# Exponentials of score tiles in two places by turns, and weight blocks loaded one tile earlier, in a fused attention and softplus-MLP kernel

## Chip, cores and metric

The kernel runs on one core of one Trainium2 chip. The metric is the device time of one launch in microseconds (us); lower is better. Engines are named as in the profile: PE is TensorE (matmuls and transposes), PEld its weight loads, DVE is VectorE, ACT is ScalarE, POOL is GpSimd, SP is the queue that issues all DMAs.

## What is computed

Attention over 8 batches with 8 heads, 576 positions and head width 64, in which scores more than `tau` below their row's maximum are dropped, and then a two-layer MLP with softplus over all 4608 tokens:

```python
scores = scale * q @ k.T                                  # per batch and head, 576 x 576
thresh = max(scores, axis=-1) - tau
attn   = softmax(where(scores >= thresh, scores, -1e9))
x      = (attn @ v) as (4608, 512)
h      = x @ w_in                                         # 512 -> 2048
g      = maximum(h, 0) + log1p(exp(-abs(h)))
out    = g @ w_out                                        # 2048 -> 512
```

`q`, `k`, `v` are float32; `w_in` and `w_out` arrive as 64-bit floats, and the kernel turns them into float32 pairs (a high and a low part) on the chip.

## The kernel before

**Attention.** There are 32 units, one for each batch and pair of heads, and each unit has 9 tiles of 128 rows of scores: 288 tiles in all, counted by `g`. A tile goes through these steps: `scores` (PE, 4 matmuls of 288 columns, 8 for the middle tile, into one of two pairs of PSUM banks), `row_max` (DVE, the negated maximum and the threshold), `exps` (ACT, line 435, from PSUM into `e_all`), `mask` (DVE, line 440: keeps what is over the threshold and sums the row), `weights_T` (PE, lines 471 to 477: transposes the masked exponentials), `weights_hi` and `weights_lo` (copies out of PSUM), and the products with `v`.

`e_all` has room for two tiles, its two halves; a tile takes the half of its parity. Tiles come in pairs (0 and 1, 2 and 3, 5 and 6, 7 and 8; tile 4 stands alone). The last 64 columns of a row of scores don't fill a block of 128. So the second tile of a pair transposes the middle 128 columns of `e_all`, which hold the remainders of both tiles, in one instruction (line 471), ahead of its own four (line 474). That instruction reads both halves. The exponentials of the next pair's first tile go into one of these halves, and so they come after it.

**The order.** The main loop walks the 288 tiles and writes out the steps of each by a string of letters. For the first 36 tiles it is `PAT0 = "RMTeShlfpfxvwp"`: row maximum of the next tile, mask of this one, transposes of this one, exponentials of the next, scores of the tile after that, and so on; `w` starts a block of weights, `v` issues three of the products with `v`, and each `p` is a point at which deferred work whose time has come is written out (two points to a tile). After that the string is `PAT`. The framework's planner then fixes the order of each engine's instructions by this order and by its own estimates of what is ready, so that an instruction can stand some tiles earlier on its engine than in the string. Every engine runs its instructions in that fixed order.

The first five units (`s.whole`, `NF = 5`) use float32 products of four passes with `v` (line 549) and need no low part, so they don't use the two buffers `gL`. MLP work (`f`) begins at tile 41; before that PE has only attention.

**Weights.** 32 blocks of 128 x 512 are loaded and split beside the first tiles. Block n is started at tile `int(W0 + n * W1)`, with `W1 = 2`: a load of 512 KB on SP (line 185) into pieces of a pool of 16; then, `WD` points later, line 193 on ACT (`first`), line 194 on POOL, lines 200, 202 and 205 on DVE some points apart, two steps on POOL (lines 125 and 132), and for `w_in` two stores to DRAM on SP (line 234).

Of the kernel before, what the change touches and what calls it, by code (L numbers as in the profile page):

```python
# [9 lines left out]
F32 = mybir.dt.float32  # L10
F32R = mybir.dt.float32r
# [12 lines left out]
P = 128  # L24
# [8 lines left out]
LAG0 = 5  # L33
PAT = "ThRlefmpfxSvwp"
PAT0 = "RMTeShlfpfxvwp"
WD = 2
ST = (1, 3, 4, 4, 5, 6, 6, 8)
VO = (1, 1, 1, 0)
RT = 1
# [12 lines left out]
NF = 5  # L52
TG = 36
W1 = 2.0
W0 = 1
SPA = 0


# [1 line left out]
def tile_kernel(ctx: ExitStack, tc: tile.TileContext, q, k, v, tau, w_in, w_out, out):  # L60
# [8 lines left out]
    nc = tc.nc  # L69
    B, H, S, D = q.shape  # L70
    NT, DM = out.shape
    DFF = w_in.shape[1]
    SM = 512
    SR = S - SM
    HS = S // 2
    NC = SM // P
# [8 lines left out]
    apool = ctx.enter_context(tc.tile_pool(name="apool", bufs=2))  # L85
# [11 lines left out]
    ident = identr.bitcast(F32)  # L97
# [52 lines left out]
    def to_f32(src, want, name, then):  # L150
# [29 lines left out]
        if src.dtype == F32:  # L180
            nc.sync.dma_start(m, src)
            later_(WD, lambda: then(parts, w, done))
            return
# [29 lines left out]

        later_(WD, first)

# [59 lines left out]
    for b in range(B):  # L275
        for kind in (("one", "two") if b < NSPLIT else ("all",)):
            for hp in range(NPAIR):
                s = Unit()
# [5 lines left out]
                for g, (j, members) in enumerate(groups):  # L284
                    c = 0
# [113 lines left out]

    e_all = cpool.tile([P, 2, S], F32, name="e_all")
    banks = [ps_s.tile([P, 2, 512], F32, tag="s", name=f"s_{i}") for i in range(SB)]
    nth = [0]

    def scores(s, t):
        if t == s.tiles[0]:
            s.sums = apool.tile([P, 9], F32, tag="sums", name=f"sums_{s.i}")
            s.half, s.sp, s.m, s.grp = {}, {}, {}, {}
        sp = banks[nth[0] % SB]  # L410
        s.half[t] = half = nth[0] % 2
        nth[0] += 1
        s.sp[t] = sp
        if t == NC:
            parts = [(qm[:, n, j, :], j) for j in range(2) for n in range(2)]
        else:
            j = 0 if t < NC else 1
            c = t if t < NC else t - NC - 1
            parts = [(s.qT[j][n][:, c * P:(c + 1) * P], j) for n in range(2)]
        k0 = (1 - half) * SR  # L420
        for m, (lhs, j) in enumerate(parts):
            for hf in range(2):
                i = nc.tensor.matmul(sp[:, hf, 0:HS], lhs, s.kT[j][:, k0 + hf * HS:k0 + (hf + 1) * HS],  # L423
                                     start=(m == 0), stop=(m == len(parts) - 1))
        scored.append(i)
# [6 lines left out]
        s.m[t] = (negm, thr)  # L432

    def exps(s, t):
        nc.scalar.activation(e_all[:, s.half[t], :].rearrange("p (h n) -> p h n", h=2), s.sp[t][:, :, 0:HS],  # L435
                             AF.Exp, bias=s.m[t][0], scale=1.0)

    def mask(s, t):
        e2 = e_all[:, s.half[t], :].rearrange("p (h n) -> p h n", h=2)
        masked.append(nc.vector.scalar_tensor_tensor(  # L440
            out=e2, in0=s.sp[t][:, :, 0:HS], scalar=s.m.pop(t)[1], in1=e2, op0=ALU.is_ge, op1=ALU.mult,
            accum_out=s.sums[:, s.tiles.index(t):s.tiles.index(t) + 1]))
# [8 lines left out]
    def mate(s, t):  # L451

        if t == NC:
            return None, False
        u = t if t < NC else t - 1
        return (t + 1, False) if u % 2 == 0 else (t - 1, True)

    def weights_T(s, t):
        half = s.half[t]
        e = e_all[:, half, :]  # L460
        other, second = mate(s, t)
        lone = other is None
        if 9 * NPAIR * s.b + 9 * s.hp + t < TG:
            main = ps_g.tile([P, NC, P], F32, tag="g", name=f"tm_{s.i}_{t}")
            rest = ps_g.tile([P, NC, P], F32, tag="g", name=f"tr_{s.i}_{t}")[:, 0, :] if lone or second else None
        else:
            sp = s.sp[t]
            main = sp[:, 0, :].rearrange("p (c n) -> p c n", n=P)
            rest = sp[:, 1, 0:P]
        if second:  # L470
            nc.tensor.transpose(rest, e_all.rearrange("p h n -> p (h n)")[:, SM:SM + P], ident)  # L471
        for c in range(NC):
            c0 = half * SR + c * P
            nc.tensor.matmul(main[:, c, :], e[:, c0:c0 + P], ident, is_transpose=True, start=True, stop=True)  # L474
        if lone:
            r0 = 0 if half else SM
            nc.tensor.transpose(rest[0:SR, :], e[:, r0:r0 + SR], ident)
        s.sp[t] = (main, rest)
# [358 lines left out]
    for kind, g in WL:  # L837
        for m in range(4):
            n = len(prep)
            prep.append((int(W0 + n * W1), prep_w_in if kind == "i" else prep_w_out,  # L840
                         (g, m) if kind == "i" else (4 * g + m,)))
# [69 lines left out]
    for n in (0, 2, 1):  # L911
        qkT(u0, 1, n)
        point()
    u0.eng, u0.eng_lo = eng, nc.gpsimd
    scores(*tiles[0])
    row_max(*tiles[0])
    exps(*tiles[0])
    scores(*tiles[1])
    for j in range(2):
        split_v(u0, j)  # L920
# [3 lines left out]
    for g, (cur, t) in enumerate(tiles):  # L924
# [5 lines left out]
        for step in PAT0 + ("m" if g == TG - 1 else "") if g < TG else PAT:  # L930
            if step == "T":
                weights_T(cur, t)
            elif step == "h":
                weights_hi(cur, t)
            elif step == "l":
                weights_lo(cur, t)
            elif step == "R" and nxt:
                row_max(*nxt)
            elif step == "e" and nxt:
                exps(*nxt)  # L940
            elif step == "m" and nxt:
                mask(*nxt)
            elif step == "M":
                mask(cur, t)
            elif step == "f":
                upto += quota / PAT.count("f")
                while done < upto:
                    done += next(ffn)
            elif step == "x":
                extras(cur.i, cur.tiles.index(t))  # L950
            elif step == "S" and g + 2 < NS:
                scores(*tiles[g + 2])
            elif step == "v":
                slow_products()
            elif step == "w":
                while prep and prep[0][0] <= g:
                    _, f, a = prep.pop(0)
                    f(*a)
            elif step == "p":
                point()  # L960
# [38 lines left out]
```

## Time and profile before

| | |
|---|---|
| median of 3 runs | 1451.85 us (1451.37 to 1452.93) |
| the profiled execution | 1450.65 us; span in the trace 1448.9 us |
| busy share of the span | PE 97%, DVE 68%, ACT 59%, POOL 41% |
| DMA moved | 189.93 MB, mean 131 GB/s |

The busy shares are means over the whole span. The first tenth of it, in which PE has only attention and the weights are prepared, differs from the rest, so the rows that matter are those of windows. PEclk is the clock that TensorE was granted, as a share of the full one.

### The profile page before, as it was taken

The numbers are of one execution on the slowest core, as the hardware profiler recorded it, in microseconds if no ns is written. First come the engines' busy times: TensorE is split into PE (matmuls) and PEld (weight loads), VectorE is DVE, ScalarE is ACT, GpSimd is POOL, SyncE is SP. The second block draws the span as 40 slices with busy tenths as digits, with TensorE's granted clock in tenths as the row PEclk, the third lists the DMA queues.
The fourth block names the chain that finished last, engine by engine and source line by source line (L and its number), as shares of the span: only waits on it lengthen the run. The fifth ranks groups of instructions, "written<-read, shape, count | busy, mean of one in ns | idle before, by whom it ended". The sixth has DMA issues, their size and how long they took to land.

```text
span 1448.9 us, 23497 instructions
## 1 busy us (share of the span) xinstructions
PE 1399.3 (97%) x7860; PEld 1161.6 (80%) x7860; DVE 983.1 (68%) x2211; ACT 848.1 (59%) x1615; POOL 591.0 (41%) x619
## 2 busy tenths in 40 slices
PE   6987999999999999999999999999999999999998
PEld 4654788878888888888888888888888888788886
DVE  6977688877777777777777777777777777402111
ACT  5766767767656566657665665667665765311010
POOL 3667666544333333344334333444334431324221
PEclk9999999999999999999999999999999999999999
DMA  5767765445333533444433533354344532344321
GB/s 160 220 192 231 212 187 170 138 121 154 109 102 110 137 115 110 119 134 150 123 111 96 153 106 101 116 151 120 113 119 136 148 98 74 101 130 129 119 85 44
DMA packets 131208, 189.93 MB, mean 131 GB/s; under 512 B 35312, under 2 KB 86800, under 8 KB 131088
## 3 DMA queue, kind: packets, MB, share of 16 engines
q1 hardware_dynamic: 131088, 188.43, 44.5%
q8 instruction: 63, 1.03, 0.3%
q14 instruction: 57, 0.47, 0.1%
HBM read 140.51 MB, written 27.41 MB: 116 GB/s over the span
## 4 chain that ended last, share of the span: by engine, by line
PE 78%; DVE 7%; ACT 5%; issue 3%; DMA 3%; POOL 2%; SPq 1%; POOLq 0%; ACTq 0%; DVEq 0%
PE s L423 10%; PE h L647 9%; PE h L645 9%; PE h L649 8%; PE o L707 8%; PE o L705 7%; PE s L474 7%; PE o L703 7%; PE pv L555 3%; PE pv L556 3%; PE tr L364 2%; DVE e_all L440 2%; DVE negm L430 2%; PE pv L549 1%; POOL g L132 1%
## 5 line engine op out<-in xcount | busy, mean ns | idle before, releaser
L132 POOL TENSOR_TENSOR g<-st,g 128x512 fp32r<-128x512 f32 x144 | 191.7, 1349 | 196.3 <-DVE g L129 182.5
L440 DVE SCALAR_TENSOR_TENSOR e_all<-s,thr,e_all 128x576 f32<-128x576 f32 x288 | 234.4, 815 | 53.0 <-ACT e_all L435 49.8
L430 DVE TENSOR_REDUCE negm<-s 128x1 f32<-128x576 f32 x288 | 217.1, 754 | 43.1 <-PE s L423 34.6
L435 ACT ACTIVATE e_all<-s,negm 128x576 f32<-128x576 f32 x288 | 215.9, 751 | 39.3 <-PE tr L471 20.7
L707 PE MATMUL o<-wo_o,g 128*128 128x512 f32 x576 | 232.3, 404 | 5.3 <-POOL g L132 5.3
L703 PE MATMUL o<-wo_o,g 128*128 128x512 f32 x576 | 232.0, 403 | 1.1 <-ACT st L667 0.7
L647 PE MATMUL h<-xl,wi 128*128 128x512 f32 x576 | 232.8, 404 | 0.0
L645 PE MATMUL h<-xh,wi 128*128 128x512 f32 x576 | 229.8, 399 | 0.0
L649 PE MATMUL h<-xh,wi 128*128 128x512 f32 x576 | 229.3, 398 | 0.0
L705 PE MATMUL o<-wo_o,g 128*128 128x512 f32 x576 | 228.5, 397 | 0.0
L498 ACT CAST gH<-s 128x512 fp32r<-128x512 f32 (+1 forms) x270 | 145.0, 550 | 139.1 <-PE s L474 135.6
L132 DVE TENSOR_TENSOR gL<-s,gH 128x512 fp32r<-128x512 f32 (+1 forms) x270 | 168.8, 634 | 47.8 <-ACT gH L498 25.3
L423 PE MATMUL s<-kT,qT 128*128 128x288 f32 x1024 | 192.2, 310 | 6.2 <-ACT gH L498 1.8
L423 PEld LDWEIGHTS s<-kT,qT 128*128 128x128 f32 x1024 | 148.5, 190 | 27.9 <-issue 11.3
L474 PE MATMUL s<-identr,e_all 128*128 128x128 f32 x1008 | 155.1, 276 | 4.8 <-DVE e_all L440 4.8
L129 DVE CAST g<-st 128x512 fp32r<-128x512 f32 x128 | 57.4, 485 | 149.5 <-ACT st L667 149.0
L667 ACT ACTIVATE st<-h 128x512 f32<-128x512 f32 x144 | 78.3, 596 | 115.3 <-PE h L649 114.6
L474 PEld LDWEIGHTS s<-identr,e_all 128*128 128x128 f32 x1008 | 114.7, 141 | 22.3 <-DVE e_all L440 12.6
L707 PEld LDWEIGHTS o<-wo_o,g 128*128 128x128 f32 x576 | 108.4, 188 | 29.1 <-POOL g L132 11.0
L645 PEld LDWEIGHTS h<-xh,wi 128*128 128x128 f32 x576 | 108.3, 188 | 23.5 <-issue 1.0
L703 PEld LDWEIGHTS o<-wo_o,g 128*128 128x128 f32 x576 | 108.5, 188 | 22.2 <-DVE g L129 2.0
L649 PEld LDWEIGHTS h<-xh,wi 128*128 128x128 f32 x576 | 108.4, 188 | 21.6
(107 smaller groups left out, 2366.4 us busy)
## 6 DMA issues: line engine op xcount, KB each, us to landing
wi<-wi_d SPq DMA_DIRECT2D x144, 512.0 KB
qT<-qT SPq DMA_DIRECT2D x124, 128.0 KB
R<-r_d SPq DMA_DIRECT2D x64, 144.0 KB
kn<-in_k_dram SPq DMA_DIRECT2D x32, 256.0 KB
qn<-in_q_dram SPq DMA_DIRECT2D x32, 256.0 KB
vn<-in_v_dram SPq DMA_DIRECT2D x32, 256.0 KB
wc_i<-in_moe_w_in_dram SPq DMA_DIRECT2D x16, 512.0 KB
wi_d<-wc_i SPq DMA_DIRECT2D x32, 256.0 KB
```

The lines of the kernel that those rows point to most:

```text
L132: eng.tensor_tensor(out=out_, in0=in_, in1=hi.bitcast(F32), op=ALU.subtract)
L423: i = nc.tensor.matmul(sp[:, hf, 0:HS], lhs, s.kT[j][:, k0 + hf * HS:k0 + (hf + 1) * HS], start=(m == 0), stop=(m == len(parts) - 1))
L430: nc.vector.reduce_max(negm, s.sp[t][:, :, 0:HS], axis=AX.XY, negate=True)
L435: nc.scalar.activation(e_all[:, s.half[t], :].rearrange("p (h n) -> p h n", h=2), s.sp[t][:, :, 0:HS], AF.Exp, bias=s.m[t][0], scale=1.0)
L440: masked.append(nc.vector.scalar_tensor_tensor(out=e2, in0=s.sp[t][:, :, 0:HS], scalar=s.m.pop(t)[1], in1=e2, op0=ALU.is_ge, op1=ALU.mult, ...
L474: nc.tensor.matmul(main[:, c, :], e[:, c0:c0 + P], ident, is_transpose=True, start=True, stop=True)
L645: nc.tensor.matmul(h, wi[:, 0, cc, :], u.h[cc], start=(cc == 0), stop=False)
L647: nc.tensor.matmul(h, wi[:, 0, cc, :], u.l[cc], start=False, stop=False)
L649: nc.tensor.matmul(h, wi[:, 1, cc, :], u.h[cc], start=False, stop=(cc == NCC - 1))
L703: nc.tensor.matmul(o, gh[:, sl], wo[fc][:, 0, :], start=(i == 0), stop=False)
L705: nc.tensor.matmul(o, gh[:, sl], wo[fc][:, 1, :], start=False, stop=False)
L707: nc.tensor.matmul(o, gl[:, sl], wo[fc][:, 0, :], start=False, stop=(i == QF - 1))
```

## The change

Three things change. The first five units put the exponentials of successive pairs by turns into `e_all` and into a second place, `e_more`, which takes one of the two `gL` buffers (`e_more` is used by units 0 to 4, `gL` from unit 5 on); each place still has two halves by parity, and mask and transposes read the place that the tile's exponentials went to. `W0` goes from 1 to 0, so that block n is loaded at tile 2n and not 2n + 1. `WD` goes from 2 to 4, so that it is taken up four points after its load and not two.

```diff
-WD = 2
+WD = 4
...
-W0 = 1
+W0 = 0
...
     e_all = cpool.tile([P, 2, S], F32, name="e_all")
+    e_more = apool.tile([P, NC, 320], F32R, tag="gL", name="e_more").bitcast(F32)
+    e_more = e_more.rearrange("p c n -> p (c n)")[:, 0:2 * S].rearrange("p (h n) -> p h n", h=2)
+    pairs = [0]
...
         sp = banks[nth[0] % SB]
         s.half[t] = half = nth[0] % 2
+        pairs[0] += not mate(s, t)[1]
+        s.e[t] = e_more if s.whole and pairs[0] % 2 else e_all
         nth[0] += 1
...
     def exps(s, t):
-        nc.scalar.activation(e_all[:, s.half[t], :].rearrange("p (h n) -> p h n", h=2), s.sp[t][:, :, 0:HS],
+        nc.scalar.activation(s.e[t][:, s.half[t], :].rearrange("p (h n) -> p h n", h=2), s.sp[t][:, :, 0:HS],
                              AF.Exp, bias=s.m[t][0], scale=1.0)
...
     def weights_T(s, t):
         half = s.half[t]
-        e = e_all[:, half, :]
+        e = s.e[t][:, half, :]
...
         if second:
-            nc.tensor.transpose(rest, e_all.rearrange("p h n -> p (h n)")[:, SM:SM + P], ident)
+            nc.tensor.transpose(rest, s.e[t].rearrange("p h n -> p (h n)")[:, SM:SM + P], ident)
```

`mask` reads `s.e[t]` in the same way.

## Rows read from the trace of the kernel before

**Rows 1.** The page, busy time of PE in the whole span.

```profile
PE 1399.3 (97%) x7860; PEld 1161.6 (80%) x7860; DVE 983.1 (68%) x2211; ACT 848.1 (59%) x1615; POOL 591.0 (41%) x619
```

**Rows 2.** Windows: stretch, length, busy time by engine, PEclk, DMA share, GB/s.

```profile
20.00:134.00 114.00, 98.11 (x557) 65.92 (x556) 95.29 (x204) 79.86 (x184) 73.21 (x87) 0.97 0.71 201
134.00:155.00 21.00, 16.90 (x80) 11.88 (x81) 13.38 (x25) 12.34 (x30) 16.05 (x19) 0.84 0.67 210
155.00:270.00 115.00, 112.54 (x629) 89.10 (x628) 92.96 (x199) 84.70 (x155) 72.06 (x80) 1.00 0.63 190
```

**Rows 3.** Waits of PE, 20 to 155 us: total, times, longest.

```profile
PE s L423 <- ACT gH L498: 4.6, 3, 2.7
PE tr L471 <- DVE e_all L440: 3.8, 6, 1.4
PE tm L474 <- DVE thr L431: 3.5, 3, 1.9
...
PE tr L471 <- DVE thr L431: 2.5, 3, 1.3
```

**Rows 4.** Waits of DVE, 20 to 155 us.

```profile
DVE e_all L440 <- ACT e_all L435: 15.3, 18, 2.9
DVE wa_o L200 <- POOL wa_o L194: 6.1, 7, 1.3
```

**Rows 5.** Waits of ACT, 20 to 155 us.

```profile
ACT e_all L435 <- PE tr L471: 20.7, 12, 3.0
ACT wa_i L193 <- DMA wc_i<-in_moe_w_in_dram: 6.9, 5, 2.8
ACT e_all L435 <- PE s L471: 3.9, 1, 3.9
...
ACT wa_o L193 <- DMA wc_o<-in_moe_w_out_dram: 2.9, 3, 1.9
```

**Rows 6.** Timeline about 90 us, three engines (idle before, and what ended it, in brackets).

```profile
87.80 3.46 PE L549 MATMUL pv<-gH,vn 128*64 128x320 f32 x6
...
91.56 0.74 ACT L435 ACTIVATE e_all<-s,negm 128x576 f32<-128x576 f32 x1 [3.02 <-PE tr L471]
...
92.33 0.82 DVE L440 SCALAR_TENSOR_TENSOR e_all<-s,thr,e_all 128x576 f32<-128x576 f32 x1 [0.97 <-ACT e_all L435]
...
95.69 1.83 PE L549 MATMUL pv<-gH,vn 128*64 128x320 f32 x6
```

**Rows 7.** Timeline of DVE, the first and the last long wait behind gated exponentials.

```profile
27.94 0.82 DVE L440 SCALAR_TENSOR_TENSOR e_all<-s,thr,e_all 128x576 f32<-128x576 f32 x1 [2.37 <-ACT e_all L435]
...
146.10 0.82 DVE L440 SCALAR_TENSOR_TENSOR e_all<-s,thr,e_all 128x576 f32<-128x576 f32 x1 [2.86 <-ACT e_all L435]
```

**Rows 8.** Timeline of ACT, DVE and PE about 133 us.

```profile
132.38 0.68 ACT L193 ACTIVATE wa_o<-wc_o 128x512 f32<-128x512 f32 x1 [1.91 <-DMA wc_o<-in_moe_w_out_dram]
...
133.82 0.82 DVE L440 SCALAR_TENSOR_TENSOR e_all<-s,thr,e_all 128x576 f32<-128x576 f32 x1 [1.18 <-ACT e_all L435]
...
134.71 0.33 PE L474 MATMUL s<-identr,e_all 128*128 128x128 f32 x1 [1.15 <-DVE e_all L440]
```

**Rows 9.** Timeline of SP and ACT: a weight block's load and its first step.

```profile
45.72 0.58 SPq L185 DMA_DIRECT2D wc_i<-in_moe_w_in_dram  x1
...
50.89 0.67 ACT L193 ACTIVATE wa_i<-wc_i 128x512 f32<-128x512 f32 x1 [1.78 <-DMA wc_i<-in_moe_w_in_dram]
```

**Rows 10.** Line 132: the first use of `gL` (count, ns min/median/max, first and last start).

```profile
L132 DVE TENSOR_TENSOR gL<-s,gH x270: 411/690/694, 174.0 to 1244.3; 128x512 fp32r<-128x512 f32 x108, 128x256 fp32r<-128x256 f32 x27
```

**Rows 11.** Groups of 20 to 134 us: count, busy us, mean ns, idle before.

```profile
L474 PEld LDWEIGHTS tm<-identr,e_all 128*128 128x128 f32 x136 | 15.0, 140 | 14.0 <-ACT qT L377 3.9 <-ACT kT L368 3.7 <-DVE e_all L440 2.3
...
L202 DVE SCALAR_TENSOR_TENSOR wa_i<-wc_i,wa_i 128x512 uint32<-128x512 uint32 x12 | 12.5, 1044 | 0.0
L205 DVE SCALAR_TENSOR_TENSOR wa_i<-wc_i,wa_i 128x512 uint32<-128x512 uint32 x12 | 10.2, 850 | 0.0
```

**Rows 12.** Lines 202 and 205 in the whole span: ns min/median/max.

```profile
L202 DVE SCALAR_TENSOR_TENSOR wa_i<-wc_i,wa_i x16: 676/940/1623, 23.8 to 196.7; 128x512 uint32<-128x512 uint32 x16
...
L205 DVE SCALAR_TENSOR_TENSOR wa_i<-wc_i,wa_i x16: 672/684/1605, 29.4 to 197.6; 128x512 uint32<-128x512 uint32 x16
```

More of the change, by code (lines that the diff above doesn't have):

```diff
@@ L408, in scores @@
             s.sums = apool.tile([P, 9], F32, tag="sums", name=f"sums_{s.i}")
-            s.half, s.sp, s.m, s.grp = {}, {}, {}, {}
+            s.half, s.sp, s.m, s.grp, s.e = {}, {}, {}, {}, {}
         sp = banks[nth[0] % SB]
         s.half[t] = half = nth[0] % 2
+        pairs[0] += not mate(s, t)[1]
+        s.e[t] = e_more if s.whole and pairs[0] % 2 else e_all
         nth[0] += 1
@@ L434, in exps @@
     def exps(s, t):
-        nc.scalar.activation(e_all[:, s.half[t], :].rearrange("p (h n) -> p h n", h=2), s.sp[t][:, :, 0:HS],
+        nc.scalar.activation(s.e[t][:, s.half[t], :].rearrange("p (h n) -> p h n", h=2), s.sp[t][:, :, 0:HS],
                              AF.Exp, bias=s.m[t][0], scale=1.0)
     def mask(s, t):
-        e2 = e_all[:, s.half[t], :].rearrange("p (h n) -> p h n", h=2)
+        e2 = s.e[t][:, s.half[t], :].rearrange("p (h n) -> p h n", h=2)
         masked.append(nc.vector.scalar_tensor_tensor(
```

## The prediction

> **What bounds the kernel now.** The page comes first: PE is busy for 97% of the span [rows 1]. So time can come only from the 3% in which it idles, or from time in which its matmuls run slow. The windows show where that is [rows 2]. From 20 to 134 us PE is busy 98.1 of 114 us, from 134 to 155 us 16.9 of 21, and from 155 to 270 us 112.5 of 115. The first two windows hold 15.9 + 4.1 = 20.0 us of idle PE. In them PE has almost only the attention of the first five units, and these are the units that the change touches. Behind 155 us PE is full: what is gained ahead of it moves the whole rest forward, and nothing in the rest gives time back.
>
> In the same windows DVE is busy 95.3 of 114 and 13.4 of 21 us [rows 2]. So PE and DVE are near to each other, both some 85% full in the long one, and each waits for the other by turns: a loop with slack for about one tile.
>
> Whom does PE wait for? For masks, mostly: its largest waits are for DVE at lines 440 and 431 (3.8, 3.5 and 2.5 us in the rows shown), and 4.6 us are scores that wait for ACT copies [rows 3]. DVE waits 15.3 us in 18 places for exponentials, and at least 6.1 us for POOL's step on a weight block [rows 4]. ACT waits 20.7 us in 12 places, and 3.9 us in one more, with an exponential in hand until PE has done line 471, the transpose that frees the place of the exponentials; and 6.9 + 2.9 us for weight blocks that have not landed [rows 5].
>
> One such place shows the chain [rows 6]. PE is in six products with `v` from 87.80 to 91.26. Only then comes line 471; ACT has waited 3.02 us for it and begins at 91.56, and the mask at 92.33 comes after 0.97 us of idle DVE.
>
> **The change, part by part.**
>
> *The second place.* The exponentials of a pair's first tile no longer wait for line 471 of the pair before: what they overwrite is a pair older. This removes ACT's 20.7 + 3.9 us of waits [rows 5]. ACT is not the bound, so what counts is the DVE idle behind them. Seven of the 18 waits of DVE follow an exponential that was so gated; they are 2.37, 0.16, 0.97, 0.43, 0.47, 0.18 and 2.86 us, 7.4 us together (the first and the last of them [rows 7], and a third [rows 6]). Not all of this reaches the end. At the first of them, at 27.94, PE was still full, so DVE's loss there was only slack lost. I take half, 3.7 us, because DVE and PE have nearly the same load and the idle of one is about as often covered by the other as not. The bounds are 0 (all of it covered) and the whole of DVE's waits for exponentials, 15.3 us [rows 4].
>
> The place itself costs nothing that I can find. No instruction is added; the exponentials, masks and transposes are as many and as large as before. `e_more` sits in a `gL` buffer, and `gL` is first written at 174.0 us by unit 5 [rows 10]. The second buffer of the two is needed two tiles after that, and by then unit 4's last pair has been transposed. Without this cover the cost would be one wait of DVE, of at most a tile (114 us for some 37 tiles, 3.1 us).
>
> *`W0` and `WD`.* By the string, block n was loaded at the end of tile 2n + 1 and taken up in the middle of tile 2n + 2. Now it is loaded at the end of tile 2n and taken up at the same point as before. So ACT's, POOL's and DVE's steps stay where they are in the string and only the load moves, by a tile, some 3 us. The loads land about 5 us after their issue: 45.72 to 50.89 us, of which ACT waited 1.78 [rows 9]. So 3 us more would cover any of ACT's waits for them (longest 2.8 us [rows 5]), if the load also stands that much earlier on SP. Behind a waiting line 193 the next exponentials are queued, and behind these the mask. At 132.38 us it is seen whole: ACT waits 1.91 us, the mask 1.18 us, PE 1.15 us [rows 8]. Three such places, this the last of them, cost DVE 1.00, 1.67 and 1.18 us, 3.85 us together. The bounds are 0 (SP's order does not change, or a store of line 234 ahead of the load still blocks SP) and 3.85 us plus POOL's part, 6.1 us [rows 4], which begins with the same late line 193: 10 us. I take a third of 3.85, 1.3 us, since the planner puts line 193 where it believes the block has landed, and it may draw line 193 forward together with the load.
>
> Each block holds its two pieces of the pool one tile longer. Counted from the code, a `w_in` block is freed at the same point as before and loaded two points earlier, so that at most three earlier blocks are in flight at a load where there were two: 8 pieces of 16, with at most 7 kept by `w_out` blocks at that stage. No further block falls to the path that does its steps at once, so I cost this at nothing. If one more did, ACT would wait a load's full 5 us in the middle of its queue [rows 9].
>
> The load itself now stands a tile earlier among SP's swaps and loads of `k`, `q`, `v`. It costs SP about 0.6 us [rows 9], as before, only at another place; I cost that at nothing, with the bound of 0.6 us at each of four units, 2.4 us.
>
> *The clock.* Granted clock is 0.97 over 114 us and 0.84 over 21 us [rows 2]: 3.4 + 3.4 = 6.8 us lost at the lower of the two levels, 1.2 GHz in place of 2.4. It fell behind gaps of PE: six products took 3.46 us at 87.80 against 1.83 us for the same six at 95.69 [rows 6], and the longest wait for ACT, 2.7 us [rows 3], lies ahead of the 0.84. Fewer gaps should give some of it back; I take 1.5 us, near a fifth, as most gaps stay.
>
> *Sum.* 3.7 + 1.3 + 1.5 = 6.5 us. The profiled execution took 1450.65 us, so 1444.15; the median of the runs lies 1.2 us above it, so the forecast is **1445.3 us**. By the bounds: gain at most 15.3 us and the clock's 6.8, cut to the 20 us that PE idles, and at least 0.
>
> **The rivals.**
>
> *DVE stays the bound (1451).* Exponentials come earlier, but DVE has its 95 of 114 us to do [rows 2], and the weight steps stretch where POOL works beside them. Lines 202 and 205 take 0.68 and 0.67 us at their shortest and 1.62 and 1.61 at their longest [rows 12]; the 24 on `w_in` blocks up to 134 us have means of 1.04 and 0.85 us [rows 11], which is 12 x 0.37 + 12 x 0.18 = 6.5 us of stretch. If DVE, freed of waits, meets POOL oftener and the stretch doubles, 6.5 us go back and the forecast's gain is gone: 1451.85 - 6.5 + 6.5, about 1451. For it speaks DVE's load; against it that POOL's work does not grow. The Trainium skill (SBUF — State Buffer, section "Who interferes with whom") says that a VectorE instruction with two SBUF inputs and a GpSimd instruction that reads SBUF exclude each other, and that the later one waits for the whole of the other. The trace agrees in the two lengths of these lines; by this rule each meeting costs up to the rest of POOL's instruction, and the result would be this rival's.
>
> *ACT's order turns against PE (1457).* This one ends on the other side. The planner, seeing exponentials ready earlier, puts them ahead of the ACT copies that free PSUM banks for the next transposes. Weight loads of line 474 already wait 3.9 us for `qT` copies and 3.7 us for `kT` copies [rows 11]. An exponential takes 0.74 us [rows 6], and there are 19 first tiles of pairs among tiles 2 to 35. If half of them push such a copy onto PE's path, that is 19 x 0.74 / 2 = 7.0 us; less the 1.3 us of the earlier loads, 1457. It decides once more than about 9 of the 19 do so while half of the gain is still there. Against it: PE was found idle mainly behind masks [rows 3], and ACT is busy only 80 of 114 us [rows 2].
>
> *All of it comes back (1437).* If DVE's 15.3 us of waits for exponentials vanish from the path whole [rows 4], the time is 1451.85 - 15.3 = 1436.6, say 1437. It needs the weight blocks in time everywhere and PE never the bound; PE's own load of 98 of 114 us [rows 2] nearly forbids it.
>
> *The loads do not move on SP.* Then the 1.3 us is missing: 1446.6, inside the likeliest case.
>
> **How the numbers follow.** Forecast's case 0.57, with its own range from 1440 to 1449; all of it 0.08; DVE stays the bound 0.18; ACT's order 0.17. A measurement of this kernel can tell about 0.2%, 2.9 us, from no change. The forecast's case and the large gain lie faster by more than that, save 0.02 of the first: faster 0.63. Within it lie the DVE rival and a little of the ACT rival: same 0.21. Slower 0.16 is the rest of the ACT rival. The range for 8 in 10 leaves out half of the large gain and a little more than half of the ACT rival: 1437 to 1455.
>
> **What would show it.** In the profile after, ACT's wait of line 435 for line 471 should be gone up to 134 us, not only smaller; DVE's waits for exponentials should fall from 15.3 to some 6 us; PE's idle of 20 us from 20 to 155 us should fall by about 5; PEclk should be nearer 1.00 there; and the start of the first MLP products should lie 5 to 7 us earlier, with the same distance kept up to the end. ACT's 9.8 us of waits for weight blocks should shrink if the loads moved. I would be wrong if line 471's wait goes and DVE then waits as long for POOL or for scores, if PE's waits for ACT copies grow, or if the gain at 155 us is lost again behind it.

## The result, and the profile after

The kernel after the change takes **1457.54 us** (median; 1453.72 to 1458.24), the kernel before 1451.85 us: ratio 1.0036, 95% interval [1.0027, 1.0046]. By the ratio that is 5.2 us slower (by the two medians 5.7) where 6.5 us of gain were forecast, and outside the range of 1437 to 1455.

The page, PE's busy time, and the same three windows as in [rows 2] (stretch, length, busy time of PE, PEld, DVE, ACT and POOL, PEclk, DMA share, GB/s):

```profile
PE 1400.2 (96%) x7860; PEld 1161.5 (80%) x7860; DVE 984.8 (68%) x2211; ACT 848.3 (58%) x1615; POOL 590.8 (41%) x619
...
20.00:134.00 114.00, 95.48 (x543) 64.48 (x541) 92.70 (x198) 77.84 (x178) 67.33 (x78) 0.96 0.69 190
134.00:155.00 21.00, 15.34 (x79) 10.07 (x79) 14.24 (x26) 12.47 (x28) 16.46 (x20) 0.92 0.52 157
155.00:270.00 115.00, 110.68 (x611) 86.65 (x611) 90.55 (x193) 80.99 (x151) 73.31 (x81) 1.00 0.67 195
```

Over the whole span PE's busy time is that of before; its idle time grew, from 15.9 + 4.1 us in the first two windows to 18.5 + 5.7, and from 2.5 to 4.3 in the third. DVE did less in the same 114 us (198 instructions, before 204): the attention fell behind. It fell behind late: the mask of tile 31 begins at 108.82 us, before at 112.37 (1.8 of these 3.6 us were won between the masks of tiles 4 and 31), and the mask of tile 36 at 129.95, before at 127.60.

The waits of ACT and of DVE, 20 to 155 us (total, times, longest). All lines from 420 on stand six further down than before: the exponentials are line 441 (before 435), the masks 446 (440), the row maxima 436 (430), the transposes 477 and 480 (471 and 474).

```profile
ACT e_more L441 <- DVE negm L436: 8.3, 9, 1.8
ACT e_all L441 <- DVE negm L436: 8.2, 8, 1.8
ACT wa_i L193 <- DMA wc_i<-in_moe_w_in_dram: 6.5, 5, 1.9
...
ACT wa_i L193 <- DMA R<-r_d: 4.8, 1, 4.8
...
ACT wa_o L193 <- DMA wc_o<-in_moe_w_out_dram: 3.3, 2, 3.1
```

```profile
DVE e_more L446 <- ACT e_more L441: 8.3, 5, 4.5
DVE wa_i L200 <- POOL wa_i L194: 6.5, 3, 3.2
DVE e_all L446 <- ACT e_all L441: 5.6, 6, 2.3
```

The wait that the change is about is gone: ACT no longer waits for the transposes of the pair before (20.7 + 3.9 us in [rows 5]). It now waits for row maxima instead, 16.5 us. But DVE still waits 8.3 + 5.6 = 13.9 us for exponentials (15.3 in [rows 4], some 6 were forecast), and ACT's waits for weight blocks, which were to shrink from 9.8 us, grew to 6.5 + 4.8 + 3.3 = 14.6. And PE's waits for copies of ACT, 4.6 us in [rows 3], grew to 11.3, two of these rows being:

```profile
PE tr L364 <- ACT xp L557: 4.7, 2, 3.4
PE s L429 <- ACT gH L504: 4.0, 2, 3.3
```

Where it is lost, the timeline shows (start, length, instruction, idle before in brackets):

```profile
105.49 0.37 SPq L234 DMA_DIRECT2D wi_d<-wc_i  x1
...
105.95 0.38 SPq L589 DMA_DIRECT2D r_d<-rt  x1
...
106.83 0.37 SPq L234 DMA_DIRECT2D wi_d<-wc_i  x1
...
107.29 0.45 SPq L185 DMA_DIRECT2D wc_i<-in_moe_w_in_dram  x1
...
107.75 0.43 DVE L200 TENSOR_SCALAR wa_i<-wa_i 128x512 uint32<-128x512 uint32 x1 [1.39 <-POOL wa_i L194]
...
113.61 0.66 ACT L193 ACTIVATE wa_i<-wc_i 128x512 f32<-128x512 f32 x1 [4.80 <-DMA R<-r_d]
...
114.57 0.54 PE L364 MATMUL tr<-identr,q 128*128 128x128 f32 x4 [3.39 <-ACT xp L557]
114.69 0.73 ACT L441 ACTIVATE e_more<-s,negm 128x576 f32<-128x576 f32 x1
114.97 1.40 POOL L599 TENSOR_TENSOR xp<-xp,R 128x576 f32<-128x576 f32 x1
115.00 1.66 DVE L200 TENSOR_SCALAR wa_i<-wa_i 128x512 uint32<-128x512 uint32 x1 [3.15 <-POOL wa_i L194]
...
118.34 0.87 PE L480 MATMUL tm<-identr,e_more 128*128 128x128 f32 x3 [3.23 <-ACT wa_i L193]
...
127.17 0.53 SPq L185 DMA_DIRECT2D wc_o<-in_moe_w_out_dram  x1
...
133.81 0.66 ACT L193 ACTIVATE wa_o<-wc_o 128x512 f32<-128x512 f32 x1 [3.06 <-DMA wc_o<-in_moe_w_out_dram]
...
135.58 0.88 PE L429 MATMUL s<-kT,qT 128*128 128x288 f32 x4 [3.32 <-ACT gH L504]
```

A weight block's load leaves SP at 107.29, behind two stores and a store of row scales. ACT stands 4.80 us at line 193 for that block (the wait is put down to the row scales' load that was issued right after it), the next exponential behind it begins at 114.69, and PE idles 3.39 and 3.23 us. (The second is put down to line 193 too; the mask that PE then needs, of tile 32, begins at 117.38, behind line 200 of 115.00.) At 133.81 the same happens with the block issued at 127.17, and PE idles 3.32 us. What SP waited for ahead of these two loads, from 95 to 135 us, and the same two blocks' loads in the kernel before:

```profile
SPq L234 <- POOL wc_i L125: 4.3, 1, 4.3
...
SPq L385 <- ACT qT L377: 4.0, 1, 4.0
```

```profile
105.24 0.46 SPq L185 DMA_DIRECT2D wc_i<-in_moe_w_in_dram  x1
...
128.04 0.54 SPq L185 DMA_DIRECT2D wc_o<-in_moe_w_out_dram  x1
```

The first load stands behind a store that waits 4.3 us for POOL, and the second behind a swap of `qT` that waits 4.0 us for a copy of ACT. The first leaves 2.1 us later than before and the second 0.9 us earlier, where both were to leave some 3 us earlier. What put them there is the question of the experiments.

### The profile page after: what moved, and what is told of

Read it like the earlier page. It is cut to its first block, busy times and chain, and to the rows that moved or that the text cites. A ratio compares the mean times of both kernels' runs of the same rounds, so it can differ in the third digit from the quotient of the medians.

```text
span 1456.1 us, 23485 instructions
## 1 busy us (share of the span) xinstructions
PE 1400.2 (96%) x7860; PEld 1161.5 (80%) x7860; DVE 984.8 (68%) x2211; ACT 848.3 (58%) x1615; POOL 590.8 (41%) x619
## 4 chain that ended last, share of the span: by engine, by line
PE 77%; DVE 6%; ACT 6%; DMA 4%; issue 3%; POOL 2%; SPq 2%; POOLq 0%; ACTq 0%; DVEq 0%
PE s L429 10%; PE h L653 8%; PE h L651 8%; PE h L655 8%; PE o L713 8%; PE o L711 7%; PE o L709 7%; PE s L480 7%; PE pv L562 3%; PE pv L561 3%; PE tr L364 2%; DVE negm L436 1%; PE pv L555 1%; DMA wc_i<-in_moe_w_in_dram 1%; ACT L673 1%
## 5 line engine op out<-in xcount | busy, mean ns | idle before, releaser
L446 DVE SCALAR_TENSOR_TENSOR e_all<-s,thr,e_all 128x576 f32<-128x576 f32 x265 | 216.0, 816 | 42.7 <-ACT e_all L441 39.5
L441 ACT ACTIVATE e_all<-s,negm 128x576 f32<-128x576 f32 x265 | 198.8, 750 | 19.6 <-DVE negm L436 17.5
L132 DVE TENSOR_TENSOR gL<-s,gH 128x512 fp32r<-128x512 f32 (+1 forms) x270 | 169.0, 634 | 46.6 <-ACT gH L504 24.2
L480 PE MATMUL s<-identr,e_all 128*128 128x128 f32 x988 | 151.3, 275 | 4.9 <-DVE e_all L446 4.8
L651 PEld LDWEIGHTS h<-xh,wi 128*128 128x128 f32 x576 | 108.3, 188 | 24.5 <-ACT xh L127 1.3
L653 PEld LDWEIGHTS h<-xl,wi 128*128 128x128 f32 x576 | 108.3, 188 | 24.3 <-POOL xl L132 3.0
```

Of the source, the lines that this page charges most:

```text
L132: eng.tensor_tensor(out=out_, in0=in_, in1=hi.bitcast(F32), op=ALU.subtract)
L441: nc.scalar.activation(s.e[t][:, s.half[t], :].rearrange("p (h n) -> p h n", h=2), s.sp[t][:, :, 0:HS], AF.Exp, bias=s.m[t][0], scale=1.0)
L446: masked.append(nc.vector.scalar_tensor_tensor(out=e2, in0=s.sp[t][:, :, 0:HS], scalar=s.m.pop(t)[1], in1=e2, op0=ALU.is_ge, op1=ALU.mult, ...
L651: nc.tensor.matmul(h, wi[:, 0, cc, :], u.h[cc], start=(cc == 0), stop=False)
L653: nc.tensor.matmul(h, wi[:, 0, cc, :], u.l[cc], start=False, stop=False)
```

## The experiments

Ratios are to the kernel before, run beside each kernel on the same chip, with 95% intervals.

### The parts alone

Three theories. A: the second place gains as forecast, and the loss comes from line 193 waiting for loads. B: the second place by itself turns ACT's order against PE (the rival of the prediction). C: any edit shakes the planner's order, and other orders are worse.

`places_only` is the change with `WD = 2` and `W0 = 1` as before:

> The changed kernel with WD and W0 back at 2 and 1: only the two places are left. Theory A (the loss comes from weight blocks: ACT reaches a block's first step before its load has landed, and the exponentials queue behind it; the second place by itself gains): faster than before by 3 to 6 us, near 1447 us, ahead of before by some 4 us at tile 31 and keeping it. Theory B (the second place itself turns ACT's order against PE, the prediction's own rival): as slow as the changed kernel, near 1457 us. Theory C (the planner's order is shaken by any edit, and no part is to blame by itself): anything from 1447 to 1457, with stalls at other tiles than in the changed kernel.

`loads_only` is the kernel before with the two constants alone:

```diff
-WD = 2
+WD = 4
...
-W0 = 1
+W0 = 0
```

> The kernel before with WD = 4 and W0 = 0 and one place: only the loads' part. Theory A: no gain, 1452 to 1457 us, since the planner puts neither the loads on SP nor their first step on ACT where the string has them; waits of line 193 for DMA stay at 10 us or more from 20 to 155 us. Theory B: 1450 to 1452 us, as this part is harmless. Theory C: anywhere within 5 us of 1452.

`after_pinned` is the change, with line 193 held behind the exponentials that stand ahead of it in the string:

```diff
-            nc.scalar.activation(m, high.bitcast(F32), AF.Abs, scale=2.0 ** 16)
+            i = nc.scalar.activation(m, high.bitcast(F32), AF.Abs, scale=2.0 ** 16)
+            if took > 1:
+                behind(i, exped)
...
```

> The changed kernel, and ACT's first step of a block (line 193) is ordered behind the exponentials written out ahead of it in the string, so that the planner can't draw it forward; nothing else. Theory A: ACT's waits for weight loads from 20 to 155 us fall from 9.8 + 4.8 us to below 4, the three stalls of PE over 3 us go, and the time is below before's: 1443 to 1449 us. Theory B: still 1455 us or more, as the exponentials keep their places. Theory C: within 5 us of 1452, with new stalls elsewhere.

`places_wd4` is the change with `W0 = 1`:

> The changed kernel with W0 back at 1: loads by the string one tile later, and taken up one tile later too (WD stays 4). Theory A: whatever lengthens the distance from a load to its first step on ACT helps, if the planner keeps that distance; 1446 to 1454 us. Theory B: near 1457 us. Theory C: within 5 us of 1452.

Measured: `places_only` 1.0034 [1.0020, 1.0048], `loads_only` 1.0002 [0.9993, 1.0012], `after_pinned` 1.0096 [1.0076, 1.0117], `places_wd4` 1.0035 [1.0021, 1.0049]. The loads alone do nothing. The places alone carry as much as the whole change, so A in its first form falls; its waits of 10 us or more in `loads_only` did not come either (line 193 waits 8.1 us there). Holding line 193 back makes it worse: in `after_pinned` its waits for loads fall from 14.6 to 5.2 us, and PE's waits for DVE grow from 7.6 to 21.0. Its time lies outside C's range too. B and C stay, C without its range.

### The place and the order, one without the other

The planner's order can be separated from the data that an instruction needs. At the end of the program every instruction of an engine is tied to the one that shall stand ahead of it, by dependences that fix the order and add no wait; the lists hold the order that the planner left in another kernel, instruction for instruction:

```diff
+    in_order(nc, tc)
...
+        chain = [rows[n] for n in order]
+        for one, two in zip(chain, chain[1:]):
+            tc.add_manual_dep(two, one.name, mybir.DependencyInfo(
+                mybir.DependencyClass.NoSync, mybir.DependencyReason.DATA), reason="order")
```

`places_exact` has two places in the order of before; `order_only` one place in the order of `places_only`; `places_rest` two places, with ACT's order from before and the other four engines' from `places_only`; `mix_actdvepe` two places, with POOL's and SP's order from before and the other three from `places_only`. Theory D is new: the missing wait itself does harm or nothing.

> Two places as in the change, WD = 2 and W0 = 1 as before, and the instructions of all five engines held in exactly the order in which they stand in the kernel before (order alone, no added wait). So only ACT's wait for the transpose is gone. The two places with the planner's own order gave 4.8 us more than before on the same chip (ratio 1.0034). Theory B (the second place is worth some 3.7 us, and the planner's new order, ACT's above all, costs 8): 3 to 5 us faster than before, ratio 0.9965 to 0.998. Theory D (the missing wait itself does the harm: exponentials run at a time that disturbs PE and DVE, or it is worth nothing): no faster than before, ratio 1.000 to 1.0035. Theory C (any other order than that of before is worse by some us, whichever engine's): as B, 0.9965 to 1.000; it parts from B in the runs below.

> The counterpart: one place as before, WD = 2 and W0 = 1, and the instructions of all five engines held in exactly the order that they have in the kernel with the two places alone. The waits of before are kept. Theory B and C: the order carries the loss, and without the second place there is nothing to set against it: 5 to 9 us slower than before, ratio 1.0035 to 1.006. Theory D: near before, ratio 0.999 to 1.001.

> Two places, ACT in exactly the order of before, and PE, DVE, POOL and SP in the order of the kernel with the two places alone. Theory B (ACT's order): the loss is gone, 0 to 5 us faster than before, ratio 0.9965 to 1.000. Theory C (other engines' order, DVE's weight steps and SP's loads): still some 4 us slower, ratio 1.002 to 1.004. Theory D: 1.000 to 1.0035.

> Two places, ACT, DVE and PE in the order of the kernel with the two places alone, POOL and SP in the order of before. Theory B: as slow as with the planner's own order, ratio 1.0025 to 1.0045. Theory C in its form that transfers and POOL's steps come at another place: near before or faster, ratio 0.997 to 1.001.

| | order of before | order of `places_only` |
|---|---|---|
| one place | 1 (before) | 1.0040 [1.0027, 1.0053] |
| two places | 1.0001 [0.9992, 1.0009] | 1.0034 [1.0020, 1.0048] |

The table settles two things. The order alone costs what the change costs, some 5.8 us, with no second place at all. And the second place is worth nothing that can be measured: 0.0001 in the one order, 1.0040 against 1.0034 in the other. B wanted a gain in `places_exact` and falls there, and C allowed for 1.000 at the most; of D the half "worth nothing" holds, and its forecast for `order_only` (near before) fails. `places_rest` came out at 1.0072 [1.0057, 1.0086] and `mix_actdvepe` at 1.0075 [1.0063, 1.0087], outside every range forecast for them: giving one or two engines back the order of before makes it worse. That the engines' orders of one plan fit each other is a likely reason and was not shown. So these two don't tell whose order it is. In the order of the change itself the second place was not priced by itself.

Why the freed wait is worth nothing is seen in `places_exact`. Its windows, and DVE's waits for exponentials from 20 to 155 us:

```profile
20.00:134.00 114.00, 96.46 (x566) 65.58 (x565) 97.66 (x207) 81.85 (x187) 74.11 (x88) 1.00 0.73 208
134.00:155.00 21.00, 16.54 (x84) 11.37 (x83) 14.08 (x28) 12.54 (x29) 15.13 (x18) 0.92 0.63 195
```

```profile
DVE e_more L446 <- ACT e_more L441: 4.2, 5, 1.2
DVE e_all L446 <- ACT e_all L441: 4.1, 6, 1.4
```

Here DVE's waits for exponentials did fall from 15.3 to 8.3 us, as the prediction wanted. PE's idle did not: 17.5 + 4.5 = 22.0 us against 20.0. And from the mask of tile 4 to that of tile 44 its trace takes 134.4 us, that of before 134.1. A reason can be read in the trace of before. The seven DVE waits of 7.4 us behind gated exponentials were followed by transposes that PE began without any idle, because it was still at other products. The first and the last of them in the kernel before, whose masks are in [rows 7]:

```profile
29.33 0.66 PE L474 MATMUL tm<-identr,e_all 128*128 128x128 f32 x4
...
147.35 0.27 PE L474 MATMUL s<-identr,e_all 128*128 128x128 f32 x1
```

No bracket stands behind either row, nor behind the other five. Where PE did wait for a mask, from 20 to 155 us, the exponential had been done for 0.5 to 2.1 us at 13 of 17 places (9.7 of 14.3 us), and the mask stood behind other work of DVE. The longest such wait, 1.86 us in [rows 3] (its releaser is put at the threshold's line), in the kernel before:

```profile
83.66 0.75 ACT L435 ACTIVATE e_all<-s,negm 128x576 f32<-128x576 f32 x1
...
84.74 0.43 DVE L200 TENSOR_SCALAR wa_o<-wa_o 128x512 uint32<-128x512 uint32 x1 [0.39 <-POOL wa_o L194]
85.08 0.75 DVE L430 TENSOR_REDUCE negm<-s 128x1 f32<-128x576 f32 x1
85.75 0.81 DVE L440 SCALAR_TENSOR_TENSOR e_all<-s,thr,e_all 128x576 f32<-128x576 f32 x1
...
86.71 0.63 PE L474 MATMUL tm<-identr,e_all 128*128 128x128 f32 x4 [1.86 <-DVE thr L431]
```

and the same tile in `places_exact`:

```profile
81.18 0.74 ACT L441 ACTIVATE e_all<-s,negm 128x576 f32<-128x576 f32 x1
...
81.87 0.43 DVE L200 TENSOR_SCALAR wa_o<-wa_o 128x512 uint32<-128x512 uint32 x1 [0.39 <-POOL wa_o L194]
82.21 0.75 DVE L436 TENSOR_REDUCE negm<-s 128x1 f32<-128x576 f32 x1
82.88 0.81 DVE L446 SCALAR_TENSOR_TENSOR e_all<-s,thr,e_all 128x576 f32<-128x576 f32 x1
...
83.84 0.63 PE L480 MATMUL tm<-identr,e_all 128*128 128x128 f32 x4 [1.86 <-DVE thr L437]
```

The exponential ended at 84.41 and the mask began at 85.75, after a weight step that waited for POOL and after the next row maximum. With two places the times of DVE's steps and of PE's wait are the same. Only the exponential begins 0.4 us nearer to them, and PE's wait does not change by it.

### What in the new order costs

On DVE the order of before never has more than two weight steps between two masks. That of `places_only` has three ahead of the masks of tiles 22 and 45 and four ahead of that of tile 28. M is a mask with its tile's number, R a row maximum, t a threshold, W a weight step (lines 200, 202, 205), a point any other instruction:

```
before       M20 WRWtRM21 WtWM22 RWtWRM23 tWM24 RWtWM25 RWtM26 R.Wt.WM27 RWtRM28
places_only  M20 RWtWM21 WRtWRWtM22 WM23 RtRWtWM24 WM25 RtM26 R.t.WM27 WRWtWRWtM28
debunch      M20 RWtWM21 WRtWM22 RWtWM23 RtRWtWM24 WM25 RtM26 R.t.WM27 WRWtM28
```

`debunch` keeps the order of `places_only` on all engines and moves six masks: those of tiles 22 and 28 to 31 ahead of one or two weight steps, so that two are left between masks there, and that of tile 45 ahead of a row maximum only. `after_exact` is the whole change in the order of `loads_only`. Theory O: the parts do next to nothing, the order carries the loss, and in `places_only` it is this bunching.

> The two places alone with the planner's own order, held on all engines as it stood, except that on DVE six masks (of tiles 22, 28, 29, 30, 31 and 45) move ahead of one or two weight steps and, twice, of the next row maximum. In that order up to four weight steps stand between two masks; in the order of before never more than two. Theory O (the loss of the two places alone, ratio 1.0034, comes from this bunching: PE waited 2.69 and 3.57 us for the masks of tiles 22 and 28 in the run of that order with one place, against 0.72 and 0.17 before): 3 to 5 us of the 4.8 come back, ratio 0.9995 to 1.0015. Rival (the bunches only mark steps that are late for another reason, and what is moved is waited for elsewhere): 1.0025 to 1.004.

> The change as it is (two places, W0 = 0, WD = 4), with the instructions of all engines held in exactly the order of the kernel that has the earlier loads alone and one place. Theory O (the parts cost and gain next to nothing by themselves, the planner's order carries the whole loss of 1.0036): ratio 0.999 to 1.001. Rival (places and earlier loads together cost in themselves, by transfers or by engines in each other's way): 1.002 to 1.004.

Measured: `debunch` 1.0002 [0.9993, 1.0010], `after_exact` 0.9995 [0.9985, 1.0006]. Both as theory O says. Moving six masks on one engine takes back the whole loss of `places_only`, while ACT's, PE's, POOL's and SP's orders stay as they were. Tile 28 in `places_only`:

```profile
100.76 0.74 ACT L441 ACTIVATE e_all<-s,negm 128x576 f32<-128x576 f32 x1
...
101.94 0.43 DVE L200 TENSOR_SCALAR wa_i<-wa_i 128x512 uint32<-128x512 uint32 x1 [2.30 <-POOL wa_i L194]
102.28 0.75 DVE L436 TENSOR_REDUCE negm<-s 128x1 f32<-128x576 f32 x1
102.95 1.27 DVE L202 SCALAR_TENSOR_TENSOR wa_i<-wc_i,wa_i 128x512 uint32<-128x512 uint32 x1
...
104.27 0.80 DVE L446 SCALAR_TENSOR_TENSOR e_all<-s,thr,e_all 128x576 f32<-128x576 f32 x1
...
105.13 0.33 PE L477 MATMUL tr<-identr,e_all 128*128 128x128 f32 x1 [3.29 <-DVE e_all L446]
```

and in `debunch`:

```profile
102.44 0.74 ACT L441 ACTIVATE e_all<-s,negm 128x576 f32<-128x576 f32 x1
...
103.21 0.82 DVE L446 SCALAR_TENSOR_TENSOR e_all<-s,thr,e_all 128x576 f32<-128x576 f32 x1 [1.94 <-ACT e_all L441]
...
104.09 0.33 PE L477 MATMUL tr<-identr,e_all 128*128 128x128 f32 x1 [0.64 <-DVE e_all L446]
```

In the first, the exponential is done at 101.50 and the mask begins 2.77 us later, behind a weight step that waits 2.30 us for POOL, a row maximum and a stretched second step. In the second, it follows its exponential at once, and PE waits 0.64 us in place of 3.29.

### Masks first, an idea that failed

If masks wait for weight steps, one may move them ahead everywhere. `before_mf` is the kernel before in its own order, with masks among tiles 5 to 33 ahead of the 18 weight steps that stood right in front of them (14 masks by its order, where the expectations say 16); `exact_mf` is the same order with two places.

> The kernel before (one place, W0 = 1, WD = 2) in its own order, except that on DVE 16 masks among tiles 5 to 35 stand ahead of the weight step that stood directly ahead of them, and the step behind the row maximum that follows. Theory: PE's waits for masks before were waits for DVE's own queue and not for exponentials; the masks of tiles 5, 11, 13, 15, 23, 30, 31 and 33 stood behind weight steps with their exponential done, and PE waited 0.35 + 0.21 + 0.61 + 1.01 + 1.86 + 1.41 + 1.07 + 1.30 = 7.8 us for them. Half to nearly all of that is gained: ratio 0.995 to 0.9975. Rival (the later weight steps hold POOL and the next row maximum up as long): 1.000 to 1.003.

> The same 16 masks ahead of their weight steps, in the same order on every engine, with two places. If the second place has a value once DVE's queue no longer stands ahead of the masks: 1 to 3 us faster than with one place, ratio 0.993 to 0.9965. If the second place is worth nothing in any order: the same as with one place, within 0.001.

Measured: 1.0037 [1.0024, 1.0051] and 1.0035 [1.0024, 1.0047]. The forecast for `before_mf` failed. PE's waits move: in its profile ACT waits 4.85 us ahead of 113.00 for a weight block, and PE idles 3.31 us ahead of 115.29 for a copy of ACT, neither of which stands in the trace of before. The trace shows how the later weight steps make that block late: line 205 begins at 106.30, now behind a mask and a row maximum; POOL waits 2.40 us for it and begins line 125 at 107.07; the store of its result leaves SP at 107.71, and the late load behind that store at 108.18, before at 105.24. Two places are worth nothing here either.

### The order of the change itself

In the change as it is only one mask, tile 32, has three weight steps ahead of it; what the profile after shows are two late loads. `after_sp` keeps its order and moves those two loads ahead on SP, the first in front of the three stores, the second in front of one store and the two swaps of `qT` behind it. `after_db` moves the mask of tile 32 alone, `after_both` does both.

> The change with its own planned order held on every engine, except that on SP two loads of weight blocks move ahead: the one issued at 107.29 us in front of the two stores and the small store of row scales that stood before it (SP stood idle there for some 4 us, waiting for POOL), and the one issued at 127.17 in front of one store. In the run of the change ACT waited 4.80 and 3.06 us for these two blocks with exponentials queued behind, and PE idled 3.39 + 3.23 and 3.32 us soon after. Theory O2 (in the change itself the loss of 5.2 us, ratio 1.0036, comes from these two loads, which the new order puts behind waiting stores): both waits go and 4 to 7 us come back, ratio 0.999 to 1.001. Rival (the loads are late, but what the order makes late next is as late): 1.002 to 1.004.

> The change with its own planned order on every engine, except that on DVE the mask of tile 32 moves ahead of the next threshold and one weight step: the only place in that order with three weight steps between two masks. Theory O2: the bunching is not what costs the change its time, ratio 1.003 to 1.004. Rival (the same cause as in the kernel with the two places alone, where moving six masks brought 1.0034 down to 1.0002): 0.9995 to 1.0015.

> Both edits at once: the two loads earlier on SP and the mask of tile 32 ahead on DVE. Theory O2: as with the loads alone, 0.999 to 1.001. Rival (two causes that must both go): 0.999 to 1.001 here, and 1.002 or more with either alone.

Measured: `after_sp` 1.0014 [1.0005, 1.0022], `after_db` 1.0033 [1.0022, 1.0045], `after_both` 1.0009 [1.0000, 1.0017]. The two loads carry most of the loss, 0.0022 of 0.0036 or some 3.2 us; the mask alone gives nothing that can be told from zero. In `after_sp`:

```profile
107.81 0.68 ACT L193 ACTIVATE wa_i<-wc_i 128x512 f32<-128x512 f32 x1
...
115.64 1.09 PE L480 MATMUL tm<-identr,e_more 128*128 128x128 f32 x4 [5.02 <-DVE e_more L446]
...
131.13 0.79 PE L429 MATMUL s<-kT,qT 128*128 128x288 f32 x4 [0.72 <-ACT gH L504]
```

Line 193 no longer waits. Of PE's 3.39 + 3.23 us there, 5.02 stay, now for the mask of tile 32 behind DVE's weight steps; of the 3.32 us at the second place, 0.72 stay. My forecast of all of it back was too high; some six tenths came. What is left in `after_both`, 0.0009, is at the edge of what can be told.

No kernel beat the one before: the best, `after_exact`, has an interval of 0.9985 to 1.0006.

## Why the prediction was wrong

- **The step that failed is the second place, 3.7 us.** I took half of 7.4 us of DVE's idle as gained, by the near balance of DVE's and PE's load. With the order of before held, the gain is 0 (`places_exact`, within 1.3 us either way). The bound of 0 was in the text, and the trace of before pointed to it: behind each of the seven waits PE began the transposes without idle. A share by load was taken where the seven rows could be followed one step further.
- **"The place itself costs nothing that I can find" left out the planner.** I counted instructions, buffers and waits, and took the order as given. The order that the planner made of the freed dependence costs 5.8 us alone (`order_only`). That an instruction can move on its engine was said in the description of the kernel, but it entered the sum only through one rival.
- **Loads, 1.3 us:** about 0 (`loads_only`, within 1.7 us). That the planner draws line 193 and SP's stores along was named as a reason to take a third; in the full change it went further: one load came to stand behind a store that waits 4.3 us for POOL, another behind a swap that waits 4.0 us for ACT.
- **Clock, 1.5 us:** no gain. After the change the granted clock is 0.96 and 0.92, before 0.97 and 0.84. In `places_exact` it is 1.00 and 0.92, and PE's idle is 2.0 us longer at the same time as before: in that execution the faster PE only waited longer. The 6.8 us from which I took a part were those of one execution: its clock over the whole span is 0.994, while the 17 runs of the kernel before beside `order_only` have a mean of 0.997. The nine runs of the change have 0.995, those of `order_only` 0.994 and of `places_exact` 0.998: the clock went down with the slow orders. How much of the loss is PE's idle and how much the lower clock of its products was not separated. The mean clock of `order_only` is 0.0033 lower than that of before; over 1457 us that is, as an estimate, at most 4.8 of its 5.8 us.
- **The rivals.** The time of "ACT's order turns against PE" was 1457, and 1457.5 came out, but not by its mechanism. In the planner's order the exponential of a tile stands ahead of the copy of the tile before at 34 of the first 36 tiles in the kernel before, at 35 in `places_only` and at 34 in the change: among these copies hardly anything could turn. (Copies of `qT` and `kT` were not counted.) The loss went with DVE's order alone in `debunch`, and mostly with SP's alone in `after_sp`. "DVE stays the bound" had the right engine for `places_only`: masks behind weight steps that wait for POOL; but its price (its own sum gives 1451.85, not 1451) was put on the steps' stretch and not on their place, and the stretch did not grow: the steps of lines 202 and 205 on `w_in` blocks up to 134 us take 1001 and 830 ns on average, before 1044 and 850 [rows 11]. "The loads do not move on SP" is what happened at two places, at a cost and not at a missing gain.
- **The signs.** The wait for line 471 went, as the text says it must; DVE's waits for exponentials (13.9, not 6), PE's idle (24.2, not 15) and ACT's waits for blocks (14.6, not below 9.8) all came out against it. The first MLP product begins at 154.0 us, before at 146.2: 7.8 us later, not 5 to 7 earlier. PE's waits for copies of ACT grew, which the text names as a sign of being wrong.

What stays open: why the planner bunches weight steps when the exponentials become ready earlier was not tried, and `places_wd4` loses 1.0035 with no bunch of three in its order. Its trace is not behind up to the mask of tile 40 (139.2 us, before 146.1); it loses behind that, where the prediction took PE as full: from 155 to 270 us PE is busy 105.2 us, before 112.5. What PE waits for there was not taken apart.

## What to carry to other kernels

Before an idle time of an engine off the path is counted as gain, follow each of its rows on to the engine that sets the end: if that one starts its next work without idle, the row gives nothing there, and whether its lateness shows at a later row a run must tell. Where a planner fixes the order, a removed dependence is also a new order on every engine, and the new order can be priced by itself, by holding the old order with the new data and the new order with the old data; do this before an effect is put down to the edit. Whole engines' orders of two plans did not mix here: giving ACT, or POOL and SP, their old order back made this kernel slower than either whole, while moving six masks or two loads within one plan won time.

## What the runs showed of the hardware

Line 200, a short step with one input, was not among the steps that the prediction saw stretch; it takes 0.43 us at 107.75 and 1.66 us at 115.00 in the profile after. At 115.00 POOL's product of line 599 had begun 0.03 us earlier and ran 1.40 us; line 200 ended after it. The kernel before shows the same at 135.66 us: 1.48 us, begun 0.07 us behind a POOL step of 1.27 us. Where line 200 begins ahead of a POOL step and none is running, as at 84.74 us (POOL's begins at 84.79), it takes its 0.43. So a step of DVE with one input can also wait for the whole of a POOL instruction. The Trainium skill (SBUF — State Buffer, section "Who interferes with whom") says that `tensor_scalar` can enter a mode with two ports, and that then the one that issues first keeps the shared ports for its whole instruction; the trace agrees in the order of the two starts and in the length. In the row at 115.00 us the weight step just behind POOL's start costs DVE 1.2 us more than its usual 0.43, and the mask of tile 32 stands behind it.
